# Grouped-query attention on one core: K of two pairs in one load, K eight pairs ahead of V

## The chip, the cores and the metric

The kernel runs on 1 core of one Trainium2 chip. The metric is the device time in microseconds (us). A core has five engines that run their own instruction streams and meet at semaphores: TensorE (PE), VectorE (DVE), ScalarE (ACT), GpSimd (POOL) and SyncE (SP), and 16 DMA engines that carry what the queues of SP and ACT issue.

## The reference

Softmax attention with 16 batches, 32 query heads, 8 key heads, 16 queries, 2048 keys and depth 128, all in bf16. Each key head serves four query heads, so for one key head there are 64 query rows.

```python
k = jnp.repeat(k, rep, axis=1)          # rep = Hq // Hkv = 4
v = jnp.repeat(v, rep, axis=1)
scores = jnp.einsum("bhqd,bhkd->bhqk", q, k) * D ** -0.5
p = softmax(scores, axis=-1)
return jnp.einsum("bhqk,bhkd->bhqd", p, v)
```

K and V are 64 MB each (counting 1 MB as 1024 x 1024 bytes); every byte is read once.

## The kernel before

The work is cut into 64 pairs of key heads (NP = 64). One pair has 1 MB of K and 1 MB of V; its 2 x 64 query rows fill 128 partitions of the scores. Step p of the pipeline does this:

- SP loads K of pair p into one of eight buffers Kn (NK = 8) and V into one of four buffers Vb (NV = 4). `copy` writes out the access patterns of a DMA by hand; `load` uses it so that two neighbouring partition rows of 8 KB are read as one row of 16 KB.
- DVE transposes K in blocks of 32 x 32 (`kt`, L482) from Kn into KT (two buffers, one pair each), with two bf16 numbers moved as one 4-byte element. Then TensorE forms the scores (`scores`, L353): 32 matmuls into four banks of PSUM.
- DVE passes over the scores twice 1024 columns (L502): it scales and negates them into Sneg, in an order that later matmuls want, and takes the row minimum. It will be called the minimum pass. POOL exchanges minima and sums between the two halves of the partitions (`exchange`).
- ACT takes the exponential (L550), TensorE transposes the probabilities (`transposes`, L371), ACT evicts them to PT (`evict`, L561), TensorE multiplies with V (`product`, L423; L412 for the last eight pairs), and ACT normalizes into an output tile (L574).

Each engine's order is written out by hand. In step p, TensorE runs scores(p+1), now and then four transposes of queries, product(p-4) (PVLAG = 4) and transposes(p). DVE runs the minimum pass of p and then `kt(p+2)`. ACT runs exp(p), norm(p-4), evict(p). The last steps are unrolled in an order of their own; there the idle matmuls of L433 (`idle`, counts IDLE = (6, 5, 3)) stand between products.

SP issues all loads in one queue in the order of this loop (L317): K of pair t, at times a chunk of queries, then V of pair t - VLAG, with VLAG = 6. A load of V waits until product(p-4) has freed its buffer (`sem_pv`); a load of K waits for the transpose that freed its buffer (`sem_kt`). SP stands at such a wait, and all later loads stand behind it. The V of the last four pairs goes into K buffers that are free by then, and the V of the last eight pairs (p >= P4 = 56) is read in two halves with another layout:

```python
for t in range(NP + VLAG):
    if t < NP:
        load_k(t)
    ...
    if 0 <= t - VLAG < NP:
        load_v(t - VLAG)
```

Outputs of the first 40 pairs (PH = 40) are stored by ACT as they come. Those of pairs 40 to 62 are held in Oh and stored by SP behind all loads, in groups HELD; pair 63 is stored by ACT at the end.

Of the kernel before, what the change touches and what calls it, by code (L numbers as in the profile page):

```python
# [11 lines left out]
NK = 8  # L12
NV = 4
# [4 lines left out]
NR = 8  # L18
VLAG = 6
PVLAG = 4  # L20
# [5 lines left out]
def bass_standalone__gqa_softmax__sampling_kernel(  # L26
# [13 lines left out]


    B, Hq, Sq, D = q.shape
    Hkv, Sk = k.shape[1], k.shape[2]
# [5 lines left out]
    P4 = NP - 8  # L49
    PH = NP - 1 - sum(HELD)  # L50
    NQC = NP // 4
    scale = float(D) ** -0.5
# [4 lines left out]

    iota_t = sb("iota_t", [128, 128], I32)
    ident4 = sb("ident4", [128, 128], F32)
    warm = sb("warm", [128, 2], F32)  # L60
    Kn = [sb(f"Kn{i}", [128, 32 * 128], BF16) for i in range(NK)]
    Vb = [sb(f"Vb{i}", [128, 32 * 128], BF16) for i in range(NV)]
    KT = [sb(f"KT{i}", [128, 32 * 64], F32) for i in range(NKT)]
    Qn = [sb(f"Qn{i}", [128, 4, 128], BF16) for i in range(NQ)]
# [5 lines left out]
    PT = [sb(f"PT{i}", [128, 8, 128], F32) for i in range(NPT)]  # L70
    Osb = [sb(f"O{i}", [128, 128], BF16) for i in range(NO)]
    Oh = sb("Oh", [128, sum(HELD), 128], BF16)

# [10 lines left out]
    sem_id = sem("sem_id")  # L84
    sem_k = [sem(f"sem_k{i}") for i in range(NK)]
    sem_v = [sem(f"sem_v{i}") for i in range(NV)]
# [24 lines left out]
    of = out.rearrange("b h s d -> (b h s) d")  # L111
    kf = k.rearrange("b h s d -> (b h s d)").rearrange("(r x) -> r x", x=4096)
    vf = v.rearrange("b h s d -> (b h s d)").rearrange("(r x) -> r x", x=4096)
# [19 lines left out]
    def v_tile(p):  # L133
        return Kn[p % 4 + (NP - 8) % NK] if p >= NP - 4 else Vb[p % NV]

    def out_tile(p, i):
        return Oh[:, p - PH, :] if isinstance(p, int) and PH <= p < NP - 1 else Osb[i % NO][:, :]

# [47 lines left out]
    with nc.Block() as block:  # L186

        @block.gpsimd
        def _(gp):
            gp.memset(warm[:, :], 0.0).then_inc(sem_id, 1)  # L190
            gp.iota(iota_t[:, :], [[1, 128]], base=0, channel_multiplier=-1).then_inc(sem_id, 1)
            gp.wait_ge(sem_id, 2)
            gp.tensor_scalar(ident4[:, :], iota_t[:, :], 0.0, None, op0=ALU.is_equal).then_inc(sem_id, 1)

# [82 lines left out]
        @block.sync  # L277
        def _(sp):
            def load_k(p):
                s = p % NK  # L280
                if p >= NK:
                    sp.wait_ge(sem_kt, p - NK + 1)
                src = kf[128 * p:128 * (p + 1), :]
                if p < 2:
                    ins = sp.dma_start(Kn[s][:, :], src)
                else:
                    ins = load(sp, Kn[s][:, :], src, 4096, 2)
                ins.then_inc(sem_k[s], 16)

            def load_v(p):  # L290
                if p >= NP - 4:
                    sp.wait_ge(sem_kt, p - 3)
                elif p >= NV:
                    sp.wait_ge(sem_pv, p - NV + 1)
                dst = v_tile(p)[:, :]
                done = sem_vx[p - NP + 4] if NP - 4 <= p < NP - 1 else sem_v[p % NV]
                if p < P4:
                    load(sp, dst, vf[128 * p:128 * (p + 1), :], 4096, 2).then_inc(done, 16)
                    return
                dst = dst.rearrange("a (g x) -> a g x", g=2)  # L300
                src = vf4[:, 2 * p:2 * p + 2, :]
                if p < NP - 1:
                    for h in range(2):
                        load(sp, dst[:, h, :], src[:, h, :], 2048, 2).then_inc(done, 16)
                    return
                for n, x in enumerate((slice(0, 1536), slice(1536, 2048))):
                    sp.dma_start(dst[:, :, x], src[:, :, x]).then_inc(sem_vl[n], 16)

            def store_held(p, n):
                sp.wait_ge(sem_nm, p + n + 1)  # L310
                src = Oh[:, p - PH:p - PH + n, :]
                copy(
                    sp, of[128 * p:128 * p + 128, :], [[128, 128], [128 * 128, n], [1, 128]],
                    src, [src.ap[0], [1, 1], [1, n * 128]],
                ).then_inc(sem_oh, 16)

            for t in range(NP + VLAG):  # L317
                if t < NP:
                    load_k(t)
                for c in range(2, NQC):  # L320
                    if t == 4 * c - QLEAD:
                        if c == NQ:
                            sp.wait_ge(sem_q4d, 2)
                        sp.wait_ge(sem_q4, max(2, 4 * c - 6))
                        load(sp, Qn[c % NQ][:, :, :], qf[512 * c:512 * (c + 1), :], 512, 2).then_inc(sem_q[c % NQ], 16)
                if 0 <= t - VLAG < NP:
                    load_v(t - VLAG)
            p = PH
            for n in HELD:
                store_held(p, n)  # L330
                p += n

        @block.tensor
        def _(pe):
# [4 lines left out]
            def scores(p, i, first=False):  # L339
                pe.wait_ge(sem_qs, p + 1)  # L340
                pe.wait_ge(sem_kt, p + 1)
                if not first:
                    pe.wait_ge(sem_max, p)
                kt = KT[i % NKT][:, :].bitcast(BF16).rearrange(
                    "p (w x b l f) -> p w b f x l", w=2, x=16, b=2, l=32)
                qs = Qs[i % 2][:, :, :].rearrange("p b (x f) -> p b f x", f=2)
                for acc in range(4):
                    b, f = divmod(acc, 2)
                    for r in range(4):
                        rows = slice(32 * r, 32 * (r + 1))  # L350
                        h = r // 2
                        for w in range(2):
                            ins = pe.matmul(  # L353
                                S_ps[64 * w:64 * (w + 1), 512 * r:512 * (r + 1)],
                                qs[rows, b, f, 64 * h:64 * (h + 1)],
                                kt[rows, w, b, f],
                                start=(acc == 0), stop=(acc == 3),
                            )
# [30 lines left out]
            def product(p, i, out, tail=False, last=False):  # L389
# [14 lines left out]
                if isinstance(p, int) and p >= P4:  # L404
                    pt = PT[i % NPT][:, :, :].bitcast(BF16).rearrange("p (h t) (w q e) -> p h w t e q", h=2, w=2, e=2)
                    vt = v_tile(p)[:, :].rearrange("p (h j d) -> p h j d", h=2, d=128)
                    for j in range(16):
                        w, t, e = j // 8, j % 8 // 2, j % 2
                        if last and j in (0, 12):
# [6 lines left out]
                else:  # L416
                    pt = PT[i % NPT][:, :, :].bitcast(BF16).rearrange("p t (w q e) -> p w t e q", w=2, e=2)
                    vt = v_tile(p if isinstance(p, int) else i)[:, :].rearrange("p (x d) -> p x d", d=128)
                    for x in range(32):
                        w, t, e = x // 16, x % 16 // 2, x % 2  # L420
                        for h in range(2):
# [50 lines left out]
        @block.vector  # L472
        def _(dve):
            def kt(p, i):
                src = Kn[i % NK][:, :].bitcast(F32)
                dst = KT[i % NKT][:, :]
                if isinstance(p, int) and p >= P4:

                    src = src.rearrange("p (m x y) -> p m x y", m=2, x=8)
                    dst = dst.rearrange("p (x m y) -> p m x y", m=2, x=8)  # L480
                dve.wait_ge(sem_k[i % NK], 2 * (p - i) + 16 * (i // NK + 1))
                ins = dve.transpose(dst, src)  # L482
                ins.then_inc(sem_kt, 1)
# [6 lines left out]
            def step(p, i):  # L490
# [4 lines left out]
                for h in range(2):  # L495
                    if not known or p < P4:
                        dst = Sneg[i % 2][:, :].rearrange("p (t h g l e) -> p h g t l e", t=8, h=2, g=2, e=2)[:, h]
                        src = S_ps[:, 1024 * h:1024 * (h + 1)].rearrange("p (g t e l) -> p g t l e", g=2, t=8, e=2)
                    else:
                        dst = Sneg[i % 2][:, :].rearrange("p (h t g l f) -> p h g t l f", h=2, t=4, g=2, f=4)[:, h]  # L500
                        src = S_ps[:, 1024 * h:1024 * (h + 1)].rearrange("p (g t f l) -> p g t l f", g=2, t=4, f=4)
                    ins = dve.tensor_scalar(  # L502
# [4 lines left out]
                if i >= 3 and i % 2:  # L507
                    recip(p - 3, i - 3, 2)
                if not known or p + 2 < NP:
                    kt(p + 2, i + 2)  # L510

# [9 lines left out]
        def _(act):  # L521
# [44 lines left out]
            def norm(p, i):  # L566
# [3 lines left out]
                if not isinstance(p, int) or p < PH:  # L570
                    act.wait_ge(sem_o[i % NO], 2 * (p - i) + 16 * (i // NO + 1))
                elif p == NP - 1:
                    act.wait_ge(sem_o[i % NO], 16 * (PH // NO + 1))
# [4 lines left out]
            def store(p, i):  # L578
                act.wait_ge(sem_nm, p + 2)
                rows = bass.ds(128 * p, 128)  # L580
                act.dma_start(of[rows, :], Osb[i % NO][:, :]).then_inc(sem_o[i % NO], 16)

# [58 lines left out]
```

## Time and profile before

| What | Value |
|---|---|
| Time, median of 3 runs | 334.62 us (334.57 to 335.05) |
| The profiled execution: its time, its span | 334.85 us, 333.5 us |
| Granted TensorE clock | 1.000 |
| Busy: PE, DVE, ACT, POOL | 279.2, 294.5, 257.7, 149.4 us |
| HBM read, written | 136.31 MB, 2.10 MB, 415 GB/s over the span |
| Packets of SP's loads (queue q1) | 98.1% of 16 engines' span |
| K load, V load: median from issue to landing | 20.2 us, 18.2 us |
| Chain that ended last | DMA 57%, PE 16%, DVE 15%, issue 8% |

The chain follows the run back from its last instruction, at each step to what released it. "Issue" is time in which an engine waited for nothing that the profile shows. A group of instructions is given with its line, engine, operation, output and input tiles and count, then its busy time, the mean of one in ns, and the idle time ahead of it with what ended most of that. A row of the rates by stretch has the window in us, its length, each engine's busy time (PE, PEld, DVE, ACT, POOL) with a count, the granted clock, the DMA share and GB/s. A timeline row has start and duration in us, then the instruction.

### The profile page before, as it was taken

How to read it: one execution, taken by the hardware profiler on the slowest of the kernel's cores; microseconds unless marked ns; L12 is line 12 of the kernel's file. 1: busy time of each engine (PE TensorE's matmuls, PEld its weight loads, DVE VectorE, ACT ScalarE, POOL GpSimd, SP SyncE). 2: the span in 40 equal slices, each digit the busy share in tenths (PEclk: the TensorE clock that was granted, in tenths of full speed). 3: DMA queues.
4: the chain of work that ended last, by engine and by line, in shares of the span. 5: the costliest groups of instructions: out<-in, count | busy, mean ns of one | idle time of the engine just before them, and what ended most of it. 6: DMA issues, size and time to landing. Idle time of an engine off the chain costs nothing.

```text
span 333.5 us, 16075 instructions
## 1 busy us (share of the span) xinstructions
PE 279.2 (84%) x6542; PEld 209.4 (63%) x6542; DVE 294.5 (88%) x354; ACT 257.7 (77%) x482; POOL 149.4 (45%) x488
## 2 busy tenths in 40 slices
PE   2585988999998999888897988979879798788877
PEld 1253756767676776666665766757757567666465
DVE  3999988999999999989898898998999999989940
ACT  3277877989898989779688787887788687776873
POOL 4444554364544555354445435354363453542320
DMA  8999999999999999999999999999999999999998
GB/s 314 426 419 422 413 419 415 431 424 422 426 423 425 420 428 420 430 418 426 422 427 420 431 419 425 424 423 425 419 421 424 415 423 421 417 425 414 412 405 293
DMA packets 19583, 138.61 MB, mean 416 GB/s; under 512 B 8432, under 2 KB 9712, under 8 KB 10864
## 3 DMA queue, kind: packets, MB, share of 16 engines
q1 hardware_dynamic: 13520, 136.95, 98.1%
q10 hardware_dynamic: 6048, 1.48, 2.0%
q8 instruction: 8, 0.13, 0.2%
q14 instruction: 7, 0.06, 0.0%
HBM read 136.31 MB, written 2.10 MB: 415 GB/s over the span
## 4 chain that ended last, share of the span: by engine, by line
DMA 57%; PE 16%; DVE 15%; issue 8%; ACT 1%; SPq 1%; POOL 1%; DVEq 0%; POOLq 0%; ACTq 0%
DMA Vb<-in_v_dram 43%; PE O_ps L423 9%; DMA Kn<-in_k_dram 8%; DVE KT L482 8%; DVE Sneg L502 7%; DMA Kn<-in_v_dram 5%; PE ST_ps L371 3%; PE S_ps L353 3%; ACT P L550 1%; SPq L173 1%; PE ST_ps L386 1%; POOL nbias L233 0%; PE ST_ps L412 0%; POOL oth L225 0%; POOL oth L228 0%
## 5 line engine op out<-in xcount | busy, mean ns | idle before, releaser
L482 DVE STREAM_TRANSPOSE KT<-Kn 128x2048 f32<-128x2048 f32 x64 | 147.7, 2308 | 20.1 <-DMA Kn<-in_k_dram 19.9
L550 ACT ACTIVATE P<-Sneg,nbias 128x1024 bf16<-128x1024 f32 x128 | 145.9, 1142 | 15.7 <-POOL nbias L233 14.2
L502 DVE TENSOR_SCALAR_CACHE_REDUCE Sneg<-S_ps 128x1024 f32<-128x1024 f32 x128 | 149.9, 1206 | 4.2 <-PE S_ps L353 4.2
L423 PE MATMUL O_ps<-Vb,PT 64*64 64x128 bf16 x3584 | 111.1, 216 | 30.5 <-issue 27.0
L423 PEld LDWEIGHTS O_ps<-Vb,PT 64*64 64x64 bf16 x3584 | 102.8, 107 | 49.3 <-issue 49.3
L561 ACT ACTIVATE PT<-ST_ps 128x512 f32<-128x512 f32 x126 | 68.5, 594 | 16.5 <-PE ST_ps L371 15.9
L353 PE MATMUL S_ps<-KT,Qs 32*64 32x512 bf16 x2048 | 73.5, 396 | 6.0 <-DVE Sneg L502 3.8
L371 PE MATMUL ST_ps<-ident,P 128*128 128x128 f32 x504 | 70.1, 283 | 8.7 <-ACT P L550 8.5
L225 POOL COPY oth<-own 64x4 f32<-64x4 f32 (+1 forms) x65 | 11.9, 183 | 136.4 <-DVE Sneg L502 134.3
L371 PEld LDWEIGHTS ST_ps<-ident,P 128*128 128x128 f32 x504 | 55.1, 143 | 16.9 <-ACT P L550 10.5
L353 PEld LDWEIGHTS S_ps<-KT,Qs 32*64 32x64 bf16 x2048 | 27.3, 106 | 30.4 <-issue 16.6
L207 POOL COPY Qs<-QT 128x512 bf16<-128x512 bf16 x64 | 39.0, 610 | 12.1 <-POOL rowsum L240 5.6
L233 POOL TENSOR_SCALAR nbias<-own,oth 128x1 f32<-128x1 f32 x128 | 33.9, 280 | 10.6 <-POOL oth L228 9.0
L163 POOL COPY Q<-Qn 128x1024 bf16<-128x1024 bf16 x31 | 32.4, 1044 | 1.4 <-DMA Qn<-in_q_dram 1.4
L574 ACT ACTIVATE O<-O_ps,rrec 128x128 bf16<-128x128 f32 x40 | 14.5, 363 | 18.7 <-PE O_ps L423 18.5
L240 POOL TENSOR_TENSOR rowsum<-own,oth 64x1 f32<-64x1 f32 x128 | 23.8, 186 | 8.2
L386 PE MATMUL ST_ps<-ident,Q 128*128 128x128 f32 x128 | 22.5, 304 | 4.6 <-POOL Q L163 4.6
L386 PEld LDWEIGHTS ST_ps<-ident,Q 128*128 128x128 f32 x128 | 14.7, 150 | 18.5 <-issue 18.5
L550 ACT ACTIVATION_READ_ACCUMULATOR P<-Sneg,nbias 128x1 f32 x128 | 24.2, 189 | 0.0
L536 ACT ACTIVATE QT<-ST_ps 128x512 f32<-128x512 f32 x32 | 18.5, 579 | 3.9 <-PE ST_ps L386 3.8
L574 ACT ACTIVATE Oh<-O_ps,rrec 128x128 bf16<-128x128 f32 x20 | 7.3, 367 | 17.3 <-PE O_ps L423 14.4
L228 POOL COPY oth<-own 64x4 f32<-64x4 f32 (+1 forms) x65 | 11.8, 181 | 7.3
(30 smaller groups left out, 44.6 us busy)
## 6 DMA issues: line engine op xcount, KB each, us to landing
Kn<-in_k_dram SPq DMA_DIRECT2D x64, 1024.0 KB, 20.2
Vb<-in_v_dram SPq DMA_DIRECT2D x56, 1024.0 KB, 18.2
Vb<-in_v_dram SPq DMA_DIRECT2D x8, 512.0 KB, 15.4
Kn<-in_v_dram SPq DMA_DIRECT2D x6, 512.0 KB, 14.5
Qn<-in_q_dram SPq DMA_DIRECT2D x15, 128.0 KB, 19.8
out_dram<-O ACTq DMA_DIRECT2D x41, 32.0 KB, 8.9
Kn<-in_v_dram SPq DMA_DIRECT2D x1, 768.0 KB, 17.7
out_dram<-Oh SPq DMA_DIRECT2D x5, 128.0 KB, 11.8
```

The source lines that it names most:

```text
L163: return eng.tensor_copy(Q4[:, :, b, :, :], src.unsqueeze(2).to_broadcast([128, 4, 4, 64]))
L207: gp.tensor_copy(Qs[i % 2][:, :, :], QT[i // 4 % 2][:, :, 128 * x:128 * (x + 1)].bitcast(BF16)).then_inc(sem_qs, 1)
L233: ins = gp.tensor_scalar(nbias[:, s, h:h + 1], own[:, s, h:h + 1], oth[:, s, h:h + 1], None, op0=ALU.min)
L240: gp.tensor_tensor(rowsum[rows, t:t + 1], own[rows, s, 2 + h:3 + h], oth[rows, s, 2 + h:3 + h], op=ALU.add,).then_inc(sem_sum[h], 1)
L353: ins = pe.matmul(S_ps[64 * w:64 * (w + 1), 512 * r:512 * (r + 1)], qs[rows, b, f, 64 * h:64 * (h + 1)], kt[rows, w, b, f], start=(acc == ...
L371: ins = pe.transpose(dst[:, 128 * t:128 * (t + 1)], P[i % 2][:, 128 * x:128 * (x + 1)], ident4[:, :])
L386: ins = pe.transpose(dst[:, 128 * j:128 * (j + 1)], src[:, j, b, :], ident4[:, :])
L423: ins = pe.matmul(out[rows, :], pt[rows, w, t, e, :], vt[rows, x, :], start=(x == 0), stop=(x == 31),)
L482: ins = dve.transpose(dst, src)
L502: ins = dve.tensor_scalar(dst, src, -scale, None, op0=ALU.mult, op1=ALU.min, accum_out=own[:, i % NR, h:h + 1],)
L550: ins = act.activation(to[:, h], of_s[:, h], ACT.Exp, bias=nbias[:, s, h:h + 1], scale=-1.0, accum_out=own[:, t, 2 + h:3 + h],)
L561: act.activation(PT[i % NPT][:, 4 * h:4 * (h + 1), :].rearrange("p t q -> p (t q)"), p_stage_ap(p, h), ACT.Copy,).then_inc(sem_ev[h], 1)
```

## The change

K of two pairs (2 MB) comes in one load into a buffer twice as long (four of them). A partition now holds 16 KB of one pair, and partitions go two by two to the first and the second pair in turn, so that a read covers 32 KB of one pair and a write 16 KB of one partition. Each of the two transposes of such a buffer handles half of the columns of both pairs; its output pattern parts the pairs, in runs of two elements. So the scores of an even pair need both transposes, and `kt` runs three pairs ahead instead of two. KT becomes as long as two pairs (two buffers), and the orders in the scores' operand, the minimum pass and the product follow the new order of the keys. The first 2 MB of K come by halves, four loads of 32 rows of 8 KB for each half. VLAG becomes 8. To make room, iota_t moves into KT[1] and the last three held outputs use the ring of output tiles instead of Oh. The waits of the last four V loads go by the transposes of whole buffers.

```diff
-VLAG = 6
+VLAG = 8
...
-    Kn = [sb(f"Kn{i}", [128, 32 * 128], BF16) for i in range(NK)]
+    Kn = [sb(f"Kn{i}", [128, 64 * 128], BF16) for i in range(NK // 2)]
...
-    KT = [sb(f"KT{i}", [128, 32 * 64], F32) for i in range(NKT)]
+    KT = [sb(f"KT{i}", [128, 64 * 64], F32) for i in range(NKT)]
+    iota_t = KT[1][:, 0:128].bitcast(I32)
...
-            def load_k(p):
-                s = p % NK
-                if p >= NK:
-                    sp.wait_ge(sem_kt, p - NK + 1)
-                src = kf[128 * p:128 * (p + 1), :]
-                if p < 2:
-                    ins = sp.dma_start(Kn[s][:, :], src)
-                else:
-                    ins = load(sp, Kn[s][:, :], src, 4096, 2)
-                ins.then_inc(sem_k[s], 16)
+            def load_k(n):
+                src = kf[128 * n:128 * (n + 1), :]
+                dst = Kn[n % (NK // 2)]
+                step = dst[:, :].ap[0][0]
+                if n == 0:
+                    for m in range(2):
+                        y = slice(4096 * m, 4096 * (m + 1))
+                        for a in range(2):
+                            for j in range(2):
+                                d, r = 2 * a + j, 64 * a + j
+                                copy(
+                                    sp, dst[d:d + 1, y], [[4 * step, 32], [1, 1], [1, 4096]],
+                                    src[r:r + 1, y], [[2 * 8192, 32], [1, 1], [1, 4096]],
+                                ).then_inc(sem_kx[m], 16)
+                    return
+                if 2 * n >= NK:
+                    sp.wait_ge(sem_kt, 2 * n - NK + 2)
+                copy(
+                    sp, dst[:, :], [[step, 128], [1, 1], [1, 8192]],
+                    src, [[2 * 8192, 32], [64 * 8192, 2], [1, 2 * 8192]],
+                ).then_inc(sem_k[n % (NK // 2)], 16)
...
-                    sp.wait_ge(sem_kt, p - 3)
+                    sp.wait_ge(sem_kt, p // 2 * 2 - 2)
...
             for t in range(NP + VLAG):
-                if t < NP:
-                    load_k(t)
+                if t < NP and t % 2 == 0:
+                    load_k(t // 2)
...
-                pe.wait_ge(sem_kt, p + 1)
+                pe.wait_ge(sem_kt, p + 2 - i % 2)
...
+                kt = KT[i // 2 % NKT][:, :].bitcast(BF16).rearrange(
+                    "p (x w z b a l f) -> p w b f a x z l", x=4, w=2, z=8, b=2, a=2, l=16)
...
             def kt(p, i):
+                n, m = divmod(i, 2)
+                src = Kn[n % (NK // 2)][:, :].bitcast(F32)[:, 2048 * m:2048 * (m + 1)]
+                dst = KT[n % NKT][:, :]
+                src = src.rearrange("p (x l a j) -> p x l a j", l=8, a=2, j=2)
+                dst = dst[:, 2048 * m:2048 * (m + 1)].rearrange("p (x a l j) -> p x l a j", a=2, l=8, j=2)
+                if n == 0:
+                    dve.wait_ge(sem_kx[m], 64)
+                elif m == 0:
+                    dve.wait_ge(sem_k[n % (NK // 2)], 2 * (p - i) + 16 * (n // (NK // 2) + (n % (NK // 2) > 0)))
                 ins = dve.transpose(dst, src)
...
-                if not known or p + 2 < NP:
-                    kt(p + 2, i + 2)
+                for n in range(2 if known and p == 0 else 3, 4):
+                    if not known or p + n < NP:
+                        kt(p + n, i + n)
```

More of the change, by code (lines that the diff above doesn't have):

```diff
@@ L50, in bass_standalone__gqa_softmax__sampling_kernel @@
     PH = NP - 1 - sum(HELD)
+    PR = NP - 1 - HELD[-1]
     NQC = NP // 4
@@ L56, in bass_standalone__gqa_softmax__sampling_kernel @@
     sem = lambda name: ctx.enter_context(nc.semaphore(name))
-    iota_t = sb("iota_t", [128, 128], I32)
     ident4 = sb("ident4", [128, 128], F32)
     warm = sb("warm", [128, 2], F32)
-    Kn = [sb(f"Kn{i}", [128, 32 * 128], BF16) for i in range(NK)]
+    Kn = [sb(f"Kn{i}", [128, 64 * 128], BF16) for i in range(NK // 2)]
     Vb = [sb(f"Vb{i}", [128, 32 * 128], BF16) for i in range(NV)]
-    KT = [sb(f"KT{i}", [128, 32 * 64], F32) for i in range(NKT)]
+    KT = [sb(f"KT{i}", [128, 64 * 64], F32) for i in range(NKT)]
+    iota_t = KT[1][:, 0:128].bitcast(I32)
     Qn = [sb(f"Qn{i}", [128, 4, 128], BF16) for i in range(NQ)]
@@ L70, in bass_standalone__gqa_softmax__sampling_kernel @@
     PT = [sb(f"PT{i}", [128, 8, 128], F32) for i in range(NPT)]
-    Osb = [sb(f"O{i}", [128, 128], BF16) for i in range(NO)]
-    Oh = sb("Oh", [128, sum(HELD), 128], BF16)
+    Osb = sb("O", [128, NO, 128], BF16)
+    Oh = sb("Oh", [128, sum(HELD[:-1]), 128], BF16)
     own = sb("own", [128, NR, 4], F32)
@@ L84, in bass_standalone__gqa_softmax__sampling_kernel @@
     sem_id = sem("sem_id")
-    sem_k = [sem(f"sem_k{i}") for i in range(NK)]
+    sem_k = [sem(f"sem_k{i}") for i in range(NK // 2)]
+    sem_kx = [sem(f"sem_kx{i}") for i in range(2)]
     sem_v = [sem(f"sem_v{i}") for i in range(NV)]
@@ L111, in bass_standalone__gqa_softmax__sampling_kernel @@
     of = out.rearrange("b h s d -> (b h s) d")
-    kf = k.rearrange("b h s d -> (b h s d)").rearrange("(r x) -> r x", x=4096)
+    kf = k.rearrange("b h s d -> (b h s d)").rearrange("(r x) -> r x", x=8192)
     vf = v.rearrange("b h s d -> (b h s d)").rearrange("(r x) -> r x", x=4096)
@@ L133, in v_tile @@
     def v_tile(p):
-        return Kn[p % 4 + (NP - 8) % NK] if p >= NP - 4 else Vb[p % NV]
+        if p < NP - 4:
+            return Vb[p % NV][:, :]
+        n = p % 4 + (NP - 8) % NK
+        return Kn[n // 2][:, 4096 * (n % 2):4096 * (n % 2 + 1)]
     def out_tile(p, i):
-        return Oh[:, p - PH, :] if isinstance(p, int) and PH <= p < NP - 1 else Osb[i % NO][:, :]
+        return Oh[:, p - PH, :] if isinstance(p, int) and PH <= p < PR else Osb[:, i % NO, :]
     def stage_ap(u):
@@ L190, in _ @@
             gp.memset(warm[:, :], 0.0).then_inc(sem_id, 1)
-            gp.iota(iota_t[:, :], [[1, 128]], base=0, channel_multiplier=-1).then_inc(sem_id, 1)
+            gp.iota(iota_t, [[1, 128]], base=0, channel_multiplier=-1).then_inc(sem_id, 1)
             gp.wait_ge(sem_id, 2)
-            gp.tensor_scalar(ident4[:, :], iota_t[:, :], 0.0, None, op0=ALU.is_equal).then_inc(sem_id, 1)
+            gp.tensor_scalar(ident4[:, :], iota_t, 0.0, None, op0=ALU.is_equal).then_inc(sem_id, 1)
             def held(p):
@@ L278, in _ @@
         def _(sp):
-            def load_k(p):
-                s = p % NK
-                if p >= NK:
-                    sp.wait_ge(sem_kt, p - NK + 1)
-                src = kf[128 * p:128 * (p + 1), :]
-                if p < 2:
-                    ins = sp.dma_start(Kn[s][:, :], src)
-                else:
-                    ins = load(sp, Kn[s][:, :], src, 4096, 2)
-                ins.then_inc(sem_k[s], 16)
+            def load_k(n):
[19 more added lines that the diff above has]
+                ).then_inc(sem_k[n % (NK // 2)], 16)
             def load_v(p):
                 if p >= NP - 4:
-                    sp.wait_ge(sem_kt, p - 3)
+                    sp.wait_ge(sem_kt, p // 2 * 2 - 2)
                 elif p >= NV:
                     sp.wait_ge(sem_pv, p - NV + 1)
-                dst = v_tile(p)[:, :]
+                dst = v_tile(p)
                 done = sem_vx[p - NP + 4] if NP - 4 <= p < NP - 1 else sem_v[p % NV]
@@ L310, in store_held @@
                 sp.wait_ge(sem_nm, p + n + 1)
-                src = Oh[:, p - PH:p - PH + n, :]
+                src = Oh[:, p - PH:p - PH + n, :] if p < PR else Osb[:, p % NO:p % NO + n, :]
                 copy(
@@ L340, in scores @@
                 pe.wait_ge(sem_qs, p + 1)
-                pe.wait_ge(sem_kt, p + 1)
+                pe.wait_ge(sem_kt, p + 2 - i % 2)
                 if not first:
                     pe.wait_ge(sem_max, p)
-                kt = KT[i % NKT][:, :].bitcast(BF16).rearrange(
-                    "p (w x b l f) -> p w b f x l", w=2, x=16, b=2, l=32)
+                kt = KT[i // 2 % NKT][:, :].bitcast(BF16).rearrange(
+                    "p (x w z b a l f) -> p w b a f x z l", x=4, w=2, z=8, b=2, a=2, l=16)
                 qs = Qs[i % 2][:, :, :].rearrange("p b (x f) -> p b f x", f=2)
@@ L355, in scores @@
                                 qs[rows, b, f, 64 * h:64 * (h + 1)],
-                                kt[rows, w, b, f],
+                                kt[rows, w, b, i % 2, f],
                                 start=(acc == 0), stop=(acc == 3),
@@ L405, in product @@
                     pt = PT[i % NPT][:, :, :].bitcast(BF16).rearrange("p (h t) (w q e) -> p h w t e q", h=2, w=2, e=2)
-                    vt = v_tile(p)[:, :].rearrange("p (h j d) -> p h j d", h=2, d=128)
+                    vt = v_tile(p).rearrange("p (h j d) -> p h j d", h=2, d=128)
                     for j in range(16):
-                        w, t, e = j // 8, j % 8 // 2, j % 2
+                        w, e, t = j // 8, j // 4 % 2, j % 4
                         if last and j in (0, 12):
@@ L417, in product @@
                     pt = PT[i % NPT][:, :, :].bitcast(BF16).rearrange("p t (w q e) -> p w t e q", w=2, e=2)
-                    vt = v_tile(p if isinstance(p, int) else i)[:, :].rearrange("p (x d) -> p x d", d=128)
+                    vt = v_tile(p if isinstance(p, int) else i).rearrange("p (x d) -> p x d", d=128)
                     for x in range(32):
-                        w, t, e = x // 16, x % 16 // 2, x % 2
+                        e, w, t = x // 16, x // 8 % 2, x % 8
                         for h in range(2):
@@ L474, in kt @@
             def kt(p, i):
[L475 to L481, printed above, removed]
+                n, m = divmod(i, 2)
[7 more added lines that the diff above has]
+                    dve.wait_ge(sem_k[n % (NK // 2)], 2 * (p - i) + 16 * (n // (NK // 2) + (n % (NK // 2) > 0)))
                 ins = dve.transpose(dst, src)
@@ L496, in step @@
                     if not known or p < P4:
-                        dst = Sneg[i % 2][:, :].rearrange("p (t h g l e) -> p h g t l e", t=8, h=2, g=2, e=2)[:, h]
-                        src = S_ps[:, 1024 * h:1024 * (h + 1)].rearrange("p (g t e l) -> p g t l e", g=2, t=8, e=2)
-                    else:
-                        dst = Sneg[i % 2][:, :].rearrange("p (h t g l f) -> p h g t l f", h=2, t=4, g=2, f=4)[:, h]
-                        src = S_ps[:, 1024 * h:1024 * (h + 1)].rearrange("p (g t f l) -> p g t l f", g=2, t=4, f=4)
+                        dst = Sneg[i % 2][:, :].rearrange("p (t h g l f) -> p h g t l f", t=8, h=2, g=2, f=4)[:, h]
+                        src = S_ps[:, 1024 * h:1024 * (h + 1)].rearrange("p (g f t l) -> p g t l f", g=2, t=8, f=4)
+                    else:
+                        dst = Sneg[i % 2][:, :].rearrange("p (h t g l f) -> p h g t l f", h=2, t=4, g=2, f=8)[:, h]
+                        src = S_ps[:, 1024 * h:1024 * (h + 1)].rearrange("p (g f t l) -> p g t l f", g=2, t=4, f=8)
                     ins = dve.tensor_scalar(
@@ L571, in norm @@
                     act.wait_ge(sem_o[i % NO], 2 * (p - i) + 16 * (i // NO + 1))
-                elif p == NP - 1:
+                elif p >= PR:
                     act.wait_ge(sem_o[i % NO], 16 * (PH // NO + 1))
@@ L580, in store @@
                 rows = bass.ds(128 * p, 128)
-                act.dma_start(of[rows, :], Osb[i % NO][:, :]).then_inc(sem_o[i % NO], 16)
+                act.dma_start(of[rows, :], Osb[:, i % NO, :]).then_inc(sem_o[i % NO], 16)
             def step(p, i):
```

## The prediction

> **What bounds the kernel now.** I read the page's busy slices first, then the rate by stretch, the DVE groups, and the end of the run on TensorE.
>
> ```profile
> DMA  8999999999999999999999999999999999999998
> GB/s 314 426 419 422 413 419 415 431 424 422 426 423 425 420 428 420 430 418 426 422 427 420 431 419 425 424 423 425 419 421 424 415 423 421 417 425 414 412 405 293
> ```
>
> The 16 DMA engines are full from the second slice to the last: the time is first byte (2.4 us) + 138.6 MB at the rate + what follows the last load. The rate depends on the shape of the packets; stretches of one shape, the last column being GB/s:
>
> ```profile
> 289.50:303.50 14.00, 11.80 (x288) 9.47 (x286) 12.39 (x18) 10.59 (x22) 4.78 (x18) 1.00 1.01 423
> 313.50:325.50 12.00, 9.55 (x209) 6.84 (x186) 6.91 (x11) 9.20 (x19) 3.99 (x19) 1.00 1.01 406
> ```
>
> The first holds 16 KB reads written as two rows of 8 KB, the second (V of the last eight pairs) 8 KB reads written as two rows of 4 KB. DVE is next in line, and waits for K:
>
> ```profile
> L482 DVE STREAM_TRANSPOSE KT<-Kn 128x2048 f32<-128x2048 f32 x64 | 147.7, 2308 | 20.1 <-DMA Kn<-in_k_dram 19.9
> L502 DVE TENSOR_SCALAR_CACHE_REDUCE Sneg<-S_ps 128x1024 f32<-128x1024 f32 x128 | 149.9, 1206 | 4.2 <-PE S_ps L353 4.2
> ```
>
> Consecutive steps of the timeline are 4.5 us apart while DVE is full (102.45 to 106.93), and 5.1 where DMA gates (20.40 us from one V landing to the fourth after it). The end, TensorE's matmuls in order of time:
>
> ```profile
> 300.74 1.98 PE L423 MATMUL O_ps<-Vb,PT 64*64 64x128 bf16 x64 [0.94 <-issue]
> 302.64 1.09 PE L371 MATMUL ST_ps<-ident,P 128*128 128x128 f32 x8
> 303.67 1.10 PE L353 MATMUL S_ps<-KT,Qs 32*64 32x512 bf16 x32
> 305.71 1.98 PE L423 MATMUL O_ps<-Vb,PT 64*64 64x128 bf16 x64 [0.95 <-issue]
> ...
> 312.89 1.12 PE L353 MATMUL S_ps<-KT,Qs 32*64 32x512 bf16 x32
> ...
> 317.94 1.11 PE L353 MATMUL S_ps<-KT,Qs 32*64 32x512 bf16 x32 [1.02 <-DVE Sneg L502]
> ...
> 329.59 0.82 PE L433 MATMUL ST_ps<-ident 128*128 128x512 bf16 x3
> 330.46 0.75 PE L412 MATMUL ST_ps<-Kn,PT 128*64 128x128 bf16 x20
> ```
>
> These are product(54), transposes(58), scores(60), product(55), then scores(62), scores(63), the last idle matmuls and product(63). TensorE has everything but V(63) ready at 330.41; the last V lands at 330.46. Loads and compute end together: any delay of the compute shows in the time.
>
> The span is 333.5 us, that execution's time 334.85, the median of the runs 334.62. I add differences in the span to the median.
>
> **Larger K packets.** 62 pairs of K go from 16 KB reads (two 8 KB rows) to 32 KB reads (two 16 KB rows). From the two stretches, a packet takes 16 x 8192 / 406 = 323 ns and 16 x 16384 / 423 = 620 ns; twice the first less the second is 26 ns fixed per packet. An engine carries 62 x 4 / 2 = 124 packets fewer: 3.2 us. Beside output stores (about 37 to 237 us, 60% of the span) the packet records of the trace show medians of 613 ns instead of 624, 11 ns less to save: 0.4 x 3.2 + 0.6 x 3.2 x 15/26 = 2.4 us. Nothing shows a 32 KB packet, so the bounds are a loss of 0.5 (two streams 1 MB apart, read in turn) and 3.2; I take 2.2, near the row of the same doubling.
>
> [...] The trace's fastest stretch is 426.
>
> **K eight pairs ahead (VLAG 6 to 8).** No bytes change, but V stands later in SP's single queue. After V(54) lands there were 12 loads of 1 MB to go (K and V alternating down to K(63), V(55) to V(63)); now the order is K(62,63), V(54), V(55) ... V(63), and 9 are left: one at 423 (2.5 us) and eight at 406 (20.7): 23.1 us. V(54) lands at 330.46 - 23.1 = 307.3 less the DMA gain; product(54) ran at 300.74. The rest of the compute is ready long before, so this landing decides: DVE, whose pass of pair 2 began at 20.76 and will begin some 3 us later (below), would reach step 58 at 24 + 56 x 4.5 = 276 us.
>
> From product(54), in TensorE's fixed order: product(54) 1.98, transposes(58) 1.05, scores(60) 1.1, product(55) 2.0 (V(55) is 2.5 us behind V(54), landed), transposes(59) 1.05, scores(61) 1.1: 8.3 us. ScalarE's eviction for pair 59 ends then, and exp(60), 2.3 us in two 1.15 halves, follows; transposes(60) ends at 11.6, scores(62) runs to 12.7. The minimum pass of pair 62 takes 2.3 with 0.3 of hand-over: scores(63) starts at 15.4. Before, 5.08 us lay between these two scores, since a transpose stood between; it is now done earlier. From scores(63) to the point where only V(63) is missing, the same work as before: 330.41 - 317.94 = 12.5. Sum 27.9 us, against 23.1 of loads: product(63) starts 4.8 us after the loads are through. The tail, hidden exactly so far, stands out by 4.8 us. If the hand-overs were 1 us shorter it would be 3.8; if longer, 5.8.
>
> **K three transposes ahead, two pairs parted.** Scores of an even pair need two transposes, but kt(p+3) in step p keeps both done a step before. K lands ahead of the V that gates, so DVE's waits for K (19.9 us) go; what is late next is V, then the scores behind product, so no step gets shorter. Queued behind that V wait on TensorE are transposes and the next scores; ScalarE and DVE wait for those.
>
> The transposes write runs of two elements; a gain is excluded, since the count stays. No row shows that pattern on a write; reads of PSUM with a step of 32 elements run at 1206 ns for 1024 elements, about one per cycle of the contiguous transposes (1.18 against 1.13 ns each). I take no cost; the cover is the 0.5 us between 4.5 and 5.1 us, a fifth of a transpose; beyond that every ns costs 64 times. The scores' operand has runs half as long: cover, TensorE's 15% idle. The minimum pass only steps differently, and the kernel already has two step patterns in one group of 1206 ns. Q loads, held outputs, iota and V(60..63) waiting on the transposes of pairs 57 and 59 cost nothing: SP comes to them after product(55).
>
> **Start.** K(0), K(1) come as eight loads of 32 rows. SP's issues take 0.6 us each (2.11 to 4.60 for four), 4.8 us in all, and 2 MB at 8 KB packets of 309 ns (the first two K loads, in the packet records) take 16 x 309 = 4.9: even; +0.2 us (0 to 0.6; no gain, as the second megabyte is awaited either way). Scores(0) must wait for the second transpose, to 11.0 instead of 8.66, and step 0 has one transpose more: compute 2 to 5 us later. The cover: 14 K and 4 V (18 MB, 45 us) are queued before V(4) waits for product(0), due near 38.
>
> Sum: 4.8 - 2.2 + 0.2 = +2.8; 334.62 + 2.8 = **337.4 us**.
>
> **Rivals.**
> *The loads still end last* (faster). Then the gain stays: 334.62 - 2.2 + 0.2 = 332.6. It decides if the chain from product(54) takes 23.1 us or less instead of 27.9. For it: 3.5 us of that stretch are idle matmuls, and "issue" gaps near 0.95 precede products. Against: the idle matmuls stand in TensorE's order, and each link has a row. 0.16.
> *K gains nothing* (the packets are cut, or two streams disturb each other): 334.62 + 4.8 + 0.2 = 339.6. For: only smaller packets are on record. 0.10.
> *The first loads run at half rate.* [...] Against: the 128-row loads show no such loss. 0.10. [...]
> *Transposes over 20% slower*: DVE becomes the bound; at 2.9 us each, 64 x (2.9 + 2.3) + 20 = 353. 0.03.
> *Terms cancel* (tail 3 us, gain 3): 334.6. 0.04.
>
> **Numbers.** The forecast has 0.57, its own range 336.0 (tail 4.3, gain 3.2) to 339.0. Slower by over 0.2% (0.7 us, what a measurement here tells from none) is 0.57 + 0.10 + 0.10 + 0.03 = 0.80. 332.4 to 340.6 takes in the forecast, no gain, cancelling and the loads ending last, 0.87; half-rate start and slow transposes are left out, and with them the outer edges of what is in.
>
> **What would show it.** Right: 32 KB packets and a K-rich rate up by 1 to 2 GB/s; hardly a wait of the transposes for K; product(54) at 305 to 306; DMA share falling 4 us before product(63), which waits for exp and eviction, not V. Wrong: a last product released by DMA, transposes above 2.4 us, or a second K load landing after 10 us.

## The result: slower by 1.3%, 1.7 us beyond the forecast

| | Before | After |
|---|---|---|
| Time, median | 334.62 us | 339.07 us (338.77 to 339.50, 4 runs) |
| The profiled execution: time, span | 334.85, 333.5 us | 339.50, 338.2 us |
| 2 MB of K landed | 8.66 us | 10.71 us |
| 4 MB landed | 13.62 us | 15.87 us |
| 118 MB of K and V landed | 305.62 us, with V(55) | 305.59 us, with K(62,63) |
| V(54) landed, product(54) started | 300.65, 300.74 us | 308.07, 308.16 us |
| Last V: most of it, the rest | 330.42, 331.10 us | 330.52, 331.18 us |
| product(63) started | 330.46 us | 335.13 us |

The ratio is 1.0131 (95% interval 1.0114 to 1.0149): +4.45 us where +2.8 was forecast. In the two profiled executions the spans differ by 4.7 us, and so do the starts of product(63). The page's slices of the changed kernel:

```profile
DMA  7999999999999999999999999999999999999993
GB/s 229 422 434 406 422 418 436 427 418 414 429 436 438 423 418 416 438 426 438 424 423 420 422 428 447 427 411 417 432 437 432 422 411 416 430 427 406 383 379 113
```

The first slice moved 229 GB/s where it was 314, the last 113 where it was 293. These are the two places where the time went; over the long stretch in between, the rate is higher than before (a single slice can read too high or too low, since a packet counts whole where it starts). The rates by stretch, the same windows of before, then of after (columns as in the prediction):

```profile
4.00:12.00 8.00, 3.88 (x40) 2.24 (x40) 5.62 (x3) 1.19 (x2) 2.57 (x4) 1.00 1.03 433
60.00:230.00 170.00, 151.51 (x3729) 115.93 (x3725) 160.62 (x193) 141.35 (x264) 81.79 (x263) 1.00 1.01 424
```
```profile
4.00:12.00 8.00, 1.94 (x8) 1.57 (x8) 3.58 (x2) 1.19 (x2) 2.57 (x4) 1.00 1.03 357
60.00:230.00 170.00, 150.97 (x3709) 115.84 (x3709) 159.49 (x193) 140.27 (x263) 80.41 (x261) 1.00 1.01 427
```

From 4 to 12 us the engines are as busy as before (share 1.03) and carry 357 GB/s instead of 433: the eight loads of 32 rows are slow by themselves, not short of work (a share can pass 1, for the same reason as above). From 60 to 230 us the rate is 424 to 427. The loads were 2.25 us behind when 4 MB had landed and level when 118 MB had, so the middle of the run won back 2.25 us in this execution.

DVE's two groups, and TensorE at the end, in order of time:

```profile
L527 DVE TENSOR_SCALAR_CACHE_REDUCE Sneg<-S_ps 128x1024 f32<-128x1024 f32 x128 | 150.9, 1215 | 24.4 <-PE S_ps L374 24.2
...
L507 DVE STREAM_TRANSPOSE KT<-Kn 128x2048 f32<-128x2048 f32 x64 | 147.2, 2301 | 4.9 <-DMA Kn<-in_k_dram 4.9
```
```profile
308.16 1.98 PE L444 MATMUL O_ps<-Vb,PT 64*64 64x128 bf16 x64 [1.44 <-issue]
310.06 1.09 PE L392 MATMUL ST_ps<-ident,P 128*128 128x128 f32 x8
311.09 1.07 PE L374 MATMUL S_ps<-KT,Qs 32*64 32x512 bf16 x32
312.09 1.98 PE L444 MATMUL O_ps<-Vb,PT 64*64 64x128 bf16 x64
...
319.25 1.07 PE L374 MATMUL S_ps<-KT,Qs 32*64 32x512 bf16 x32
...
322.94 1.13 PE L374 MATMUL S_ps<-KT,Qs 32*64 32x512 bf16 x32 [0.19 <-DVE Sneg L527]
...
334.38 0.82 PE L454 MATMUL ST_ps<-ident 128*128 128x512 bf16 x3
335.13 1.08 PE L433 MATMUL ST_ps<-Kn,PT 128*64 128x128 bf16 x32
```

The transposes are no slower (2301 ns against 2308) and hardly wait for K any more (4.9 us in two waits at the start, instead of 19.9). That idle time is now in the minimum pass, waiting for scores (24.2 us instead of 4.2): the scores stand behind product in TensorE's order, and product waits for V. The timeline shows product(54), transposes(58), scores(60), product(55), then scores(62), scores(63), the last idle matmuls and product(63). Product(63) starts 26.97 us after product(54), and 4.61 us after most of the last V landed, where before it started with that landing.

### The profile page after: what moved, and what is told of

It is laid out like the page before. It is cut to its first block, busy times and chain, and to the rows that moved or that the text cites. A ratio compares the mean times of both kernels' runs of the same rounds, so it can differ in the third digit from the quotient of the medians.

```text
span 338.2 us, 16050 instructions
## 1 busy us (share of the span) xinstructions
PE 279.6 (83%) x6542; PEld 210.2 (62%) x6542; DVE 294.5 (87%) x354; ACT 257.6 (76%) x482; POOL 150.2 (44%) x488
## 4 chain that ended last, share of the span: by engine, by line
DMA 55%; PE 23%; DVE 11%; issue 6%; ACT 3%; SPq 1%; POOL 1%; DVEq 0%; POOLq 0%; ACTq 0%
DMA Vb<-in_v_dram 53%; PE O_ps L444 11%; DVE Sneg L527 6%; DVE KT L507 5%; PE S_ps L374 5%; PE ST_ps L392 4%; ACT P L576 3%; DMA Kn<-in_k_dram 2%; SPq L181 1%; PE ST_ps L407 1%; PE ST_ps L454 1%; POOL nbias L241 0%; ACT PT L587 0%; PE S_ps L392 0%; PE ST_ps L433 0%
## 5 line engine op out<-in xcount | busy, mean ns | idle before, releaser
L527 DVE TENSOR_SCALAR_CACHE_REDUCE Sneg<-S_ps 128x1024 f32<-128x1024 f32 x128 | 150.9, 1215 | 24.4 <-PE S_ps L374 24.2
L576 ACT ACTIVATE P<-Sneg,nbias 128x1024 bf16<-128x1024 f32 x128 | 145.9, 1143 | 19.9 <-POOL nbias L241 19.0
L507 DVE STREAM_TRANSPOSE KT<-Kn 128x2048 f32<-128x2048 f32 x64 | 147.2, 2301 | 4.9 <-DMA Kn<-in_k_dram 4.9
L374 PE MATMUL S_ps<-KT,Qs 32*64 32x512 bf16 x2048 | 74.9, 400 | 10.7 <-DVE KT L507 6.7
L374 PEld LDWEIGHTS S_ps<-KT,Qs 32*64 32x64 bf16 x2048 | 28.5, 107 | 35.3 <-issue 24.4
```

The source lines that it names most:

```text
L374: ins = pe.matmul(S_ps[64 * w:64 * (w + 1), 512 * r:512 * (r + 1)], qs[rows, b, f, 64 * h:64 * (h + 1)], kt[rows, w, b, i % 2, f], start=( ...
L527: ins = dve.tensor_scalar(dst, src, -scale, None, op0=ALU.mult, op1=ALU.min, accum_out=own[:, i % NR, h:h + 1],)
L576: ins = act.activation(to[:, h], of_s[:, h], ACT.Exp, bias=nbias[:, s, h:h + 1], scale=-1.0, accum_out=own[:, t, 2 + h:3 + h],)
```

## Experiments

Each experiment is an edit of the kernel before or after, and the quoted text is what was expected before it ran. These texts count the kernels in the order of the runs; that number stands in each heading here. Times are medians; the kernel before took 334.53 us beside kernels 1 to 4, 334.77 beside 5 to 8 and 334.64 beside 9 to 11. Landing times and packets are read from the one profiled execution of each kernel.

**The tail: K eight pairs ahead, alone (kernel 1).** The kernel before, with

```diff
-VLAG = 6
+VLAG = 8
```

> The kernel before with VLAG = 8 and nothing else: V two places later in SP's queue, K loads, packets and start as before. Theory (the order of the loads is what costs): the loads still end at about 330.5, but after V(54) only 10 loads instead of 12 are left (25.6 us), while the chain from product(54) to product(63) takes 27 us (measured in the changed kernel) and 1 to 2 us more where transposes of K still stand between the passes; product(63) starts 1.5 to 4.2 us after the last V, time 336.1 to 338.8, and no wait of product(63) on DMA. Rival (the coarser K loads and the parted transposes cost, not the order): 334.6 within 0.3, product(63) still released by V.

Measured: 338.24 us (338.06 to 338.40), ratio 1.011 (1.0094 to 1.0125). V(54) landed at 305.48, most of the last V at 330.27, and TensorE's end reads:

```profile
305.56 1.98 PE L423 MATMUL O_ps<-Vb,PT 64*64 64x128 bf16 x64 [0.94 <-issue]
...
333.88 1.09 PE L412 MATMUL ST_ps<-Kn,PT 128*64 128x128 bf16 x32
```

No other part of the change is in this kernel, and product(63) stands 3.6 us behind the loads: 24.8 us of loads after V(54) against a chain of 28.3. The order of the loads alone makes the tail stick out.

**The tail: without its idle matmuls (kernel 5).** The changed kernel, with

```diff
-IDLE = (6, 5, 3)
+IDLE = (0, 0, 0)
```

> The changed kernel without the idle matmuls (IDLE 0, 0, 0); nothing of the result hangs on them. Theory (the chain of compute behind V(54) sets the end): the idle matmuls of 1.25 and 0.82 us right before the last two products stand in that chain, product(63) comes about 2 us sooner, still behind the last V at 330.5 and not released by it: 337.1 (336.6 to 337.8). Rival (loads or stores set the end): 339.1 within 0.4. If the matmuls run at a lower clock without them: 339 or more, with longer matmuls in the tail.

Measured: 337.33 us (336.88 to 337.99), ratio 1.0075 (1.0063 to 1.0087), so about 1.7 us less than the changed kernel. The last V landed at 330.39, as before this edit, and product(63) came earlier:

```profile
332.67 0.86 PE L433 MATMUL O_ps<-Kn,PT 128*64 128x128 bf16 x24 [0.60 <-issue]
333.37 1.06 PE L433 MATMUL ST_ps<-Kn,PT 128*64 128x128 bf16 x32
```

Product(63) is 1.76 us sooner; 0.44 of that is V(54), which landed sooner in this execution (307.63), and 1.32 is the chain itself, now 25.65 us. Less work on TensorE, with the loads ending where they did, gives a shorter run: the chain of compute sets the end, not the loads.

**The start: eight loads of 32 rows, alone (kernel 6).** The kernel before, with K(0) and K(1) each as four loads of 32 rows, partitions four apart:

```diff
-                    ins = sp.dma_start(Kn[s][:, :], src)
+                    for d in range(4):
+                        copy(
+                            sp, dst[d:d + 1, :], [[4 * step, 32], [1, 1], [1, 4096]],
+                            src[d:d + 1, :], [[4 * 4096, 32], [1, 1], [1, 4096]],
+                        ).then_inc(sem_kx[p], 16)
```

> The kernel before with its first two K loads as four loads of 32 rows each, partitions four apart, as in the change; all else as before. Theory (these loads cost 2 us of the DMA engines, and in a kernel that they bound it all shows at the end): K(1) lands at 10.7 instead of 8.7, the last V at 332.5, time 336.6 (336.2 to 336.9). Rival (the loss is made up later, or belongs to the changed kernel alone): 334.5 within 0.3.

Measured: 336.81 us (336.33 to 337.20), ratio 1.0059 (1.0047 to 1.0071): +2.0 us. K(1) landed at 10.75 instead of 8.66, the last V at 332.23, and product(63) started at 332.27. Of the 2.1 us lost at the start 1.8 arrive at the end, since the loads never pause.

**The start: 32 neighbouring partitions (kernel 10).** The same, with other partitions in each load:

```diff
-                            sp, dst[d:d + 1, :], [[4 * step, 32], [1, 1], [1, 4096]],
-                            src[d:d + 1, :], [[4 * 4096, 32], [1, 1], [1, 4096]],
+                            sp, dst[32 * d:32 * d + 1, :], [[step, 32], [1, 1], [1, 4096]],
+                            src[32 * d:32 * d + 1, :], [[4096, 32], [1, 1], [1, 4096]],
```

> The kernel before with its first two K loads as four loads of 32 neighbouring partitions each, the same number and size of loads as in the sixth kernel, other partitions. [...] Rival (the number of small loads costs, not their partitions): K(1) at 10.7 and 336.8 as in the sixth kernel. If neighbours are free of collisions: K(1) near 8.7 and 334.6.

Measured: 339.30 us (339.05 to 339.89), ratio 1.0140 (1.0124 to 1.0156): +4.7 us. K(1) landed at 13.51, 4.85 us later than before. The stretch from 4 to 12 us, of the experiment with partitions four apart and then of this one:

```profile
4.00:12.00 8.00, 3.81 (x40) 2.23 (x40) 3.53 (x2) 1.20 (x2) 2.36 (x4) 1.00 0.97 340
```
```profile
4.00:12.00 8.00, 2.71 (x24) 2.02 (x32) 2.31 (x1) 1.19 (x2) 2.43 (x4) 1.00 1.07 235
```

All engines are busy (a share of 1.07) at 235 GB/s. In the packet records the 256 packets of 8 KB of the first 2 MB have a median of 589 ns, where the kernel before has 309; in the changed kernel the median is 309 still, but the mean is 424 (330 before), and one in ten takes 750 or more. So here, at the same number and size of loads, the partitions that a load reaches (and with them the rows of K that it reads) set the rate: 235 GB/s from 4 to 12 us with neighbours, where nearly all packets are slow, and 340 with partitions four apart, where some are. How many varies from one execution to the next: with eight loads to the same partitions K(1) landed between 9.84 and 10.83 us in six profiled executions (kernels 3 to 6, 11 and the changed one), with a mean of 380 to 424 ns a packet. What makes these packets slow, no run here shows.

**The start: the first 2 MB in one load (kernels 2 and 8).** The changed kernel without its case for n == 0, so that the first two pairs come as all others do, in 32 KB reads over 128 partitions:

```diff
-                if n == 0:
-                    for m in range(2):
...
-                    return
...
-                if n == 0:
-                    dve.wait_ge(sem_kx[m], 64)
-                elif m == 0:
+                if m == 0:
```

> The changed kernel with its first 2 MB of K in one load like the others instead of eight loads of 32 rows. Theory (the eight loads lose 2 us of the DMA engines, and all that follows is shifted by it): the first K has landed by 8.7 instead of 10.7, V(54) at 306.0 instead of 308.1, time 337.0 (336.6 to 337.6). Rival (the shift at the start is absorbed, since compute has slack and the tail is set by something else): 339.1 within 0.4.

Measured: 339.98 us (338.06 to 341.53, 5 runs), ratio 1.0176 (1.0158 to 1.0193). In the profiled execution, which was the shortest of the five, K(0) and K(1) landed at 9.34, V(54) at 306.22 (1.85 earlier than in the changed kernel), the last V at 328.55 and product(63) started at 333.30: span 336.3, 1.9 less. That profile bears the theory out; the median doesn't. Part of the difference lies outside the span: in kernels 2, 7 and 8, whose first 2 MB come in one load, the time is 1.7 to 1.8 us more than the span in every execution, in all others 1.3 to 1.4. What these 0.4 us are, no trace shows. The same kernel was run again to see what spreads the times:

> The kernel of the second experiment once more, since its five times spread from 338.06 to 341.53 while its profiled execution, the fastest, had product(63) 1.8 us sooner than the change. If the spread belongs to the kernel: again times between 338 and 341.5, and a profiled execution that is slow shows where the time goes (DMA rate, clock, or a wait). If it was chance: 337.0 to 338.1.

Measured: 338.69 us (338.20 to 340.20), ratio 1.0112 (1.0097 to 1.0127). This time the profiled execution was the longest. Its granted clock by slice, and product(54) in it:

```profile
PEclk9999799999999999999999999999999999997999
```
```profile
306.77 3.52 PE L433 MATMUL O_ps<-Vb,PT 64*64 64x128 bf16 x64 [1.92 <-issue]
```

One slice near 308 us is at 0.7, product(54) takes 3.52 us instead of 1.98, and product(55) starts at 312.35 where the first profile had 310.25; 0.46 of these 2.1 us is V(54), which landed later. TensorE had stood idle for 1.92 us when product(54) began (1.21 in the first profile); in all the profiles from 20 us on the clock dipped only behind a gap of 1.88 us or more (the last section has the count). Product(63) follows at 335.44, though most of the last V landed at 330.74. The chain from product(54) to it took 28.67 us instead of 26.99: this dip, in the tail, is paid in full (1.54 us in product(54)), because compute sets the end there. What made the other long runs long was not profiled, and the mean clock does not tell (339.88 at 1.00), so the cause of their spread stays open.

**The packets: reads of 16 KB again (kernel 4).** The changed kernel, each partition's 16 KB read by itself, in the order of memory. The keys of two pairs are then mixed, so the output is that of other keys:

```diff
-                    src, [[2 * 8192, 32], [64 * 8192, 2], [1, 2 * 8192]],
+                    src, [[8192, 128], [1, 1], [1, 8192]],
```

> The changed kernel with K read in rows of 16 KB in their own order, one per partition, so 16 KB reads and 16 KB writes instead of 32 KB reads and two 16 KB writes; the keys of the two pairs are mixed by it, so the kernel computes something else with the same instructions. Theory (a fixed cost per packet of some 10 to 23 ns): the 2.2 us that the middle of the run had gained go, 341.2 (340.5 to 342). Rival (the cost hangs on the rows written): no change, 339.1 within 0.4, V(54) still at 308.

Measured: 339.55 us (339.08 to 339.71), ratio 1.0144 (1.0128 to 1.0160), with V(54) at 308.27 and product(63) at 335.35, each 0.2 us later than in the changed kernel. Undoing the larger reads, my explanation of the gain, costs at most 0.5 us of 2.2. By the packet records the loads took 286.5 us from the 4th MB to the 118th before, 284.1 in the changed kernel (2.4 less; by the landings above it was 2.25), and 284.2 to 284.9 in its four variants that leave these packets as they are (kernels 2, 3, 5 and 8); here they took 284.8, so a loss is not clear of that scatter. The rival held as far as this run goes: the gain does not hang on the size of the reads.

**The packets: reads of 32 KB, written in rows of 8 KB (kernel 11).** The other half of that pair:

```diff
-                    sp, dst[:, :], [[step, 128], [1, 1], [1, 8192]],
+                    sp, dst[:, :], [[step, 128], [4096, 2], [1, 4096]],
```

> The changed kernel with each K partition written as two rows of 8 KB while reads stay at 32 KB; same result. Theory after the fourth kernel (what costs is the row written, some 10 ns each, not the packet read): the gain of the middle goes, V(54) lands at 309.5 to 310.3 instead of 308.1, time 340.4 to 341.3. Rival (32 KB reads alone carry the gain, and the fourth kernel had another reason): 339.1 within 0.4.

Measured: 341.29 us (340.87 to 341.32), ratio 1.0191 (1.0178 to 1.0204), with V(54) at 309.85 and product(63) at 336.92, 1.8 us later than in the changed kernel. The loads took 286.0 us from the 4th MB to the 118th. With the large reads kept and the written rows as short as before, most of the gain is gone. The median durations of packets between 60 and 230 us, from the packet records, per 32 KB of K (in the first and third row V's packets of 16 KB, which are the same in all four kernels, are counted with K's):

| Reads, written rows | ns per 32 KB |
|---|---|
| before: 2 reads, 4 rows of 8 KB | 2 x 614 = 1228 |
| 1 read, 4 rows of 8 KB | 1227 |
| 2 reads, 2 rows of 16 KB | 2 x 611 = 1222 |
| after: 1 read, 2 rows of 16 KB | 1214 |

From 250 to 300 us, without output stores, the four are 1250, 1246, 2 x 619 = 1238 and 1227. K's packets of the third alone, told from V's by the landings between which they started, have a median of 615 there, so 1230. Without stores, then, the longer rows save some 20 ns (1250 to 1230, 1246 to 1227) and the larger read 3 or 4; beside the stores it is 6 and 13 for the rows, 1 and 8 for the read. What is left open is small: the changed kernel reads from two places 1 MB apart in turn and kernel 4 does not, so a gain from larger reads and a loss from that order may cancel.

**Seven pairs ahead (kernel 3).** The changed kernel with VLAG = 7:

> The changed kernel with VLAG = 7. Theory: V(54) goes ahead of K(62,63), so it lands some 5 us sooner, and K(62,63) becomes what the tail waits for; of the 4.6 us that stand out behind the last V some 1.8 go: 337.3 (336.6 to 338.2). Rival (K must be eight pairs ahead, since transposes run three pairs ahead): DVE waits for K in every second step and the time stays or grows, 339 or more.

Measured: 338.72 us (337.02 to 339.57), ratio 1.0133 (1.0117 to 1.0148). In the profiled execution, the shortest (span 335.7), V(54) landed at 302.28 and V(55) at 309.66, product(55) at 309.75 gated the rest, the last V landed at 329.77, and product(63) started at 332.66, 2.9 us behind. The profile is as the theory had it, helped by a start in which K(1) landed at 9.84 instead of 10.71; the median is 1.4 us above it, with mean clocks of 0.975 in two of the longer runs. Half shown.

**All mends together (kernel 7).** One load for the first 2 MB, VLAG = 7 and no idle matmuls:

> The changed kernel with its first K in one load, VLAG = 7 and no idle matmuls. Theory, from the profiles: product(63) came at 332.7 with VLAG = 7, less 2 for the start and 1 to 2 for the idle matmuls, so 329 to 330, at or just behind the last V (327.7): 333 to 334.3, the gain of the larger loads showing at last. Rival (the one load at the start brings back what made the second experiment spread, 338.1 to 341.5): 335.5 or more, spread by over 1 us.

Measured: 339.35 us (337.94 to 342.11), ratio 1.0144 (1.0111 to 1.0178). The theory fell. V(4) was issued only at 45.69, after product(0); the K and V queued ahead of it had run out by then. The page gives the sixth slice 246 GB/s, and the stretch from 42 to 60 us has a DMA share of 0.83 and 325 GB/s (after: 1.02 and 423). With VLAG = 7 there are 2 MB, 4.9 us, fewer ahead of V(4), and the single load makes DVE wait for all 2 MB before its first transpose. Neither alone did this: DMA kept its rate from 42 to 60 us with VLAG = 7 and eight loads (416 GB/s) and with one load and VLAG = 8 (421). The granted clock was low here too, 0.90 from 34 to 42 us and 0.88 from 42 to 50, and its part is not told apart.

The last version (kernel 9) keeps VLAG = 7 and no idle matmuls, with the first K as four loads of 64 rows, partitions two apart:

> The changed kernel with VLAG = 7, no idle matmuls, and the first 2 MB of K as four loads of 64 rows (partitions two apart, two loads for each half) instead of eight of 32. Theory: the start loses less (K(1) at 9 to 10 instead of 10.7) and the first transpose need not wait for 2 MB, so V(4) is issued by 42 and DMA does not run dry as in the seventh kernel; product(63) at 329 to 331, time 333.4 to 335. Rival (64 rows collide like 32, or the clock of TensorE dips on the path): 335.5 to 338.

Measured: 336.86 us (335.50 to 340.18, 8 runs), ratio 1.0065 (1.0031 to 1.0099). K(1) landed at 10.26, which lies among the times of the eight loads (9.84 to 10.83). From 42 to 50 us DMA still runs low, the first row here; the second is the same stretch with VLAG = 7 and eight loads (kernel 3):

```profile
42.00:50.00 8.00, 8.00 (x200) 6.07 (x196) 7.54 (x9) 7.10 (x15) 3.45 (x15) 1.00 0.93 365
```
```profile
42.00:50.00 8.00, 7.14 (x155) 5.01 (x155) 8.00 (x10) 7.57 (x16) 3.73 (x15) 1.00 1.03 425
```

Product(0) started at 41.18 us where kernel 3 had 39.72, and V(4) was issued at 43.37 instead of 41.73. From 34 to 42 us, ahead of that, the granted clock was 0.79, in kernel 3 it was 1.00:

```profile
34.00:42.00 8.00, 5.71 (x100) 3.31 (x86) 8.00 (x9) 5.35 (x10) 5.12 (x15) 0.79 1.03 434
```

So the time fell where the rival had it, and a dip of the clock on the path fits; no second profile tests it. V(54) landed at 304.77, 2.5 us later than in kernel 3, and most of the last V only at 332.00, with product(63) at 333.03. No version tried beats the kernel before; the changed kernel with VLAG = 6 was not among them.

## Why the prediction was right, and where it was off

*The sign and the mechanism were right.* The K ahead of V turned a tail hidden behind the loads into one that stands out. The step "product(63) starts 4.8 us after the loads are through" measured 4.61: the loads after V(54) took 22.45 us (forecast 23.1), the chain 26.97 (forecast 27.9). Its links also hold: scores(62) began 11.09 us after product(54) (forecast 11.6), scores(63) at 14.78 (15.4), and from there to product(63) 12.19 (12.5). VLAG alone and the kernel without idle matmuls show that this is the cause, and the rival with loads that end last is out. The time by itself would not tell: 339.07 lies just outside the forecast's own range (336.0 to 339.0) and is nearer to the 339.6 of the rival in which K gains nothing. That rival is out by the rate, 427 GB/s instead of 424 from 60 to 230 us, and by the packets of K.

*The term that was mis-sized is the start.* I called eight loads of 32 rows "even" with 2 MB at packets of 309 ns, and took +0.2. It was 2.05 us at K(1) and 2.25 at 4 MB. With it went the sign "product(54) at 305 to 306": it came at 308.16. The packet time was carried over from a load that reaches all 128 partitions. The rival "the first loads run at half rate" had the direction: half rate is an estimated 4.9 us more for 2 MB (16 packets an engine at 309 ns), the 32 neighbouring partitions lost 4.85, and the changed kernel lost 2.05. At 4 MB the start cost 2.05 us more than forecast, and the tail, 4.57 us longer than before instead of 4.8, gave 0.2 back: that is the miss between the two profiled executions (product(63) 4.67 us later against +2.8). The sign of being wrong set for it, "a second K load landing after 10 us", is what the trace shows, and kernel 6 shows it alone.

*The gain from larger packets had the right size and, for the most part, the wrong reason.* Forecast 2.2, regained 2.25. I priced it as 26 ns for each packet that is read; the two experiments put most of it on the rows written. The row that I worked from changes both at once (16 KB reads in two 8 KB rows, 8 KB reads in two 4 KB rows), so it could not give the cause; the size came out because the change doubles reads and rows together too. The best long stretch of the changed kernel, from 60 to 230 us, has a mean of 427 GB/s. The prediction's "fastest stretch", 426, was not the fastest before: from 4 to 12 us it moved 433. (Its 5.08 us between scores(62) and scores(63) before are 5.05 by the rows that it shows; nothing hangs on it.)

*The steps costed at nothing held.* Transposes with runs of two elements measured 2301 ns (2308), the minimum pass 1215 (1206), scores with half as long runs 400 ns a matmul (396). DVE's waits for K went where the prediction had them go, to V and the scores behind product.

*The cover of the start held, with less to spare.* Product(0) was forecast due near 38 us. It ended at 42.97. The clock was at 0.62 from 34 to 42 us in that execution; with VLAG = 7 and the clock at 1.00 it started 1.3 us sooner, but K(1) had landed 0.87 us sooner there too, so the part of the clock is not told apart. V(4) was issued near 43 and DMA did not pause. The prediction gave 45 us as the point where that cover ends. In the kernel with all mends, with V(4) issued at 45.69 and 2 MB less ahead of it, that cover was lost and DMA ran low.

## What to carry to other kernels

When loads are reordered ahead of one another, count what is left to load after the operand that the last chain of compute waits for, and compare it with that chain: here 22.5 us of loads leave some 4.5 us of a chain of 27 uncovered. When a load is split, look at which partitions each part reaches, not only at bytes and packet size: here 8 KB packets took a mean of 577 ns with 32 neighbours and 380 to 424 with 32 partitions four apart. An explanation taken from rows in which two things change together needs a run for each of them before it is used elsewhere.

## What was not expected of the hardware

- The rate of these loads went with their set of partitions: for 8 KB packets a mean of 330 ns over 128 partitions, 380 to 424 with 32 partitions four apart (six executions), 388 with 64 two apart (one execution, not to be told from the former), and 577 with 32 neighbours.
- Splitting what is written cost more than splitting what is read: without output stores, 32 KB of K went from 1227 to 1246 ns when written in four rows instead of two, and to 1230 when read in two parts instead of one.
- In these profiles a dip of the granted clock was half the clock for 3.4 us or twice that, which a slice of 8 us shows as 0.6 to 0.9. From 20 to 330 us the 13 profiles have 19 dips. Each started within 1.4 us of the end of a gap in which TensorE stood idle for 1.88 us or more; there were 36 such gaps. None followed the 97 gaps of 1.3 to 1.85 us. No run changes such a gap alone, so that the gap causes the dip is not shown.
- What a dip cost depended on where it fell. The one from 33 to 40 us in the changed kernel left DMA at its pace (a share of 1.01 from 34 to 42 us). The one near 308 us in kernel 8, behind the last gating V, made product(54) 1.54 us longer, and product(63) came later by that.
